# The up scheme on twelve gate tiles instead of eight, one VectorE add for two in each output pair, and half of the last rotation moved back

## The chip, the cores and the metric

The kernel runs on one core of one Trainium2 chip. The metric is device microseconds (us) of one execution. A profiled execution gives a trace, and its *span* is some 1.8 us shorter than the time. TensorE is the matmul engine (PE in the views, PEld its weight loads), VectorE is DVE, ScalarE is ACT, GpSimd is POOL.

## The reference, cut to what matters

The output is `x + A(xn) + B(xn)` with `xn = layernorm(x)`, for 2048 tokens of 512 values:

```python
# A: a diagonal complex state-space layer, B: a gated MLP
for t in range(L):
    h = Lam_bar[None, :] * h + Bu[:, t, :]          # Bu = xn times B_bar
y = 2.0 * einsum("blp,dp->bld", hseq, Cmat).real + x * Dskip
gate, up = xn @ w1, xn @ w3                         # 512 -> 1792 each
out = (silu(gate) * up) @ w2                        # 1792 -> 512
```

Of the kernel before, what the change touches and what calls it, by code (L numbers as in the profile page):

```python
# [11 lines left out]
ALU = mybir.AluOpType  # L12
ACT = mybir.ActivationFunctionType

FP32 = DT.float32
BF16 = DT.bfloat16
FP16 = DT.float16
P = 128
# [4 lines left out]
class Filler:  # L23
# [8 lines left out]
    def add(self, cost, fn, key=None):  # L32
        self.tasks.append((cost, fn, key))
# [30 lines left out]
def kernel(  # L64
# [17 lines left out]
    nc = tc.nc  # L82
    _, S, D = A_x.shape
    F = B_w1.shape[1]
    PS = A_Lambda_re.shape[0]
    CPB = 4
    TBLK = CPB * P
    NCH = S // P
    NBLK = NCH // CPB
# [3 lines left out]
    LN_EPS = 1e-5  # L93
    FIRST = 3
    MID = 8
    NG = 2
    TH = TBLK // 2
    LEAD = 2.0
    LATER = (4, 5)
# [2 lines left out]
    DH = D // 2  # L102
    NFH, NPH = NFT // 2, NPT // 2
    NK = NFH + 2 * NPH
    D1, D2 = slice(0, DH), slice(DH, D)
# [5 lines left out]

    ctx.enter_context(tc.manual_schedule())
    const = ctx.enter_context(tc.tile_pool(name="const", bufs=1))
    xpool = ctx.enter_context(tc.tile_pool(name="xpool", bufs=NBLK))
    lnp = ctx.enter_context(tc.tile_pool(name="lnp", bufs=2))
    xtp = ctx.enter_context(tc.tile_pool(name="xtp", bufs=2))
    glup = ctx.enter_context(tc.tile_pool(name="glup", bufs=3))
# [2 lines left out]
    ssmw = ctx.enter_context(tc.tile_pool(name="ssmw", bufs=2))  # L120
# [26 lines left out]
    tabe = const.tile([P, NPT, 3, TBLK], BF16, name="tabe")  # L147


    x_blk = [xpool.tile([P, CPB, D], BF16, name="x_blk") for _ in range(NBLK)]  # L150
    w1v = B_w1.rearrange("(t p) f -> p t f", p=P)
    w3v = B_w3.rearrange("(t p) f -> p t f", p=P)

# [56 lines left out]
    bg = Filler(LEAD)  # L210
# [99 lines left out]
    gp = nc.gpsimd  # L310
# [112 lines left out]
    def act_state(b, hf):  # L423
        k = k_state(2 * hf)
        return act(b)[:, k:k + 4, :].rearrange("p (j r) t -> p j r t", r=2)
# [21 lines left out]
    def ssm_tasks(b, posts_last=False, between=(), middle=(), late=()):  # L447
        FULL = [P, 2, 2, TBLK]

        def half(hf):  # L450
            psl = slice(2 * hf, 2 * hf + 2)
            st = {}

            def pre_a():
                if b == 0:
                    sin_step((2 * hf + 1, 1))
                    nc.vector.tensor_scalar(out=tabe[:, psl, 2, :], in0=tabe[:, psl, 1, :], scalar1=-1.0,
                                            scalar2=None, op0=ALU.mult)
                st["g"] = u_blk[b, hf]
                if (b, hf) in ((2, 1), (3, 0)):  # L460
                    st["p"] = x_blk[b].rearrange("p (j r) t -> p j r t", r=2)
                elif b == NBLK - 1:
                    st["p"] = xtp.tile([P, NDT, TBLK], BF16, name="xnT").rearrange("p (j r) t -> p j r t", r=2)
                else:
                    st["p"] = ssmw.tile(FULL, BF16, name="p")
                nc.vector.tensor_tensor(out=st["p"][:, :, ::-1, :], in0=st["g"], in1=tabe[:, psl, 2:0:-1, :],
                                        op=ALU.mult)

            def pre_b():
                nc.vector.tensor_tensor(out=st["g"], in0=st["g"], in1=tabe[:, psl, 0:1, :].to_broadcast(FULL),  # L470
                                        op=ALU.mult)

            def pre_c():
                if b == 0 or (b, hf) == (2, 0):
                    nc.vector.tensor_tensor(out=st["g"], in0=st["g"], in1=st["p"], op=ALU.add)
                else:
                    gp.dma_start(out=st["g"], in_=st["p"], accum_op=ALU.add)

            def scan(j, ri):
                pt = 2 * hf + j  # L480
                init = 0.0
                if b in (1, 2):
                    init = ends[:, hf, 2 * j + ri:2 * j + ri + 1]
                elif b > 2:
                    init = act_blk[b - 1][:, k_state(pt, ri), TBLK - 1:TBLK]
                v = st["g"][:, j, ri, :]
                nc.vector.tensor_tensor_scan(out=v, data0=rho[:, pt:pt + 1].to_broadcast([P, TBLK]), data1=v,  # L487
                                             initial=init, op0=ALU.mult, op1=ALU.add)

            def post_a():  # L490
                st["p"] = ssmw.tile(FULL, BF16, name="p")
                st["p16"] = st["p"].bitcast(FP16)
                nc.vector.tensor_tensor(out=st["p16"][:, :, ::-1, :], in0=st["g"], in1=tabe[:, psl, 1:3, :],  # L493
                                        op=ALU.mult)

            def post_b():
                nc.vector.tensor_tensor(out=act_state(b, hf), in0=st["g"],  # L497
                                        in1=tabe[:, psl, 0:1, :].to_broadcast(FULL), op=ALU.mult)

            def post_c():  # L500
                if (b, hf) == (NBLK - 1, 1):
                    nc.vector.tensor_tensor(out=act_state(b, hf), in0=act_state(b, hf), in1=st["p16"], op=ALU.add)
                else:
                    gp.dma_start(out=act_state(b, hf), in_=st["p16"], accum_op=ALU.add)  # L504

            if (b, hf) == (1, 1):
                pre_c.ready = lambda: ("squares", 2, CPB - 1) in sins_done
            pre_a.ready = lambda: (b, hf) in u_blk
            scans = [lambda j=j, ri=ri: scan(j, ri) for j in range(2) for ri in range(2)]
            return (pre_a, pre_b, pre_c), scans, (post_a, post_b, post_c)  # L510

        (pre0, scans0, post0), (pre1, scans1, post1) = (half(hf) for hf in range(NPT // 2))

        transfers = (post0[2],) + (() if b == NBLK - 1 else (post1[2],)) + ((pre1[2],) if b > 0 else ()) + ((pre0[2],) if b in (1, 3) else ())

        def add(*fns):
            for fn in fns:
                bg.add(0.0 if fn in transfers else 1.2, fn, ("scan", b) if fn in scans0 else ("ssm", b))

        if b == 0:  # L520
            add(*pre0, *scans0, *post0, *pre1, *scans1, *post1)
            return
        add(*pre0)
        for t in middle:
            bg.add(*t)
        add(*pre1)
        for t in between:
            bg.add(*t)
        add(*scans0)
        for t in late:  # L530
            bg.add(*t)
        if posts_last:
            add(*scans1)
            return lambda: add(*post0, *post1)
        add(*post0, *scans1, *post1)


    def glu(b):
# [320 lines left out]
        for t in res_list(b):  # L859
            bg.add(*t)  # L860

    def res_difference(b):
        def difference():
            o = xn_blk[b]
            nc.vector.tensor_tensor(out=o[:, 0::2, D2].bitcast(FP16), in0=o[:, 0::2, D2], in1=o[:, 1::2, D2],
                                    op=ALU.subtract)

        bg.add(0.4, difference, ("res", b))

    def weight_state(kh, dsl):  # L870
        return ct[:, kh * NPH:(kh + 1) * NPH, :, dsl].rearrange("p a r d -> p (a r) d")
# [27 lines left out]
    def sum_homes():  # L899
        n = NK * P  # L900
        spare = tw[:, 3, :, :].rearrange("p k d -> p (k d)")
        xs = [x_blk[i].rearrange("p c d -> p (c d)") for i in range(2)]
        q = [v[:, n:n + 2 * DH].bitcast(FP32) for v in xs]
        q.append(const.tile([P, DH], FP32, name="q2"))
        return [[v[:, 0:n] for v in xs], [spare[:, 0:n], spare[:, n:2 * n]]], q

    sums = {}
# [45 lines left out]
    def y_fast(n, then=(), between=()):  # L953
        b, p = pairs[n]
        last = n == len(pairs) - 1
        bg.flush(("sums", n))
        bg.flush("tw")
        if p == 0 and b > 1:
            bg.flush(("scan", b + 1))
        c1 = 2 * p  # L960
        v = sums[n]
        res = xn_blk[b]
        g, halves, f, z = seeded[n]
        q0 = x_blk[2].rearrange("p c d -> p (c d)")[:, 0:2 * DH].bitcast(FP32) if n == 5 else q[0]
        tsum = [weight(0, D2, True)] + [[tw[:, i, k, :] for k in range(NK)] for i in range(3)]
        o1, o2 = res[:, c1, :], res[:, c1 + 1, :]
# [12 lines left out]
        def add(out, x, w):  # L979
            bg.own(0.35)  # L980
            nc.vector.tensor_tensor(out=out, in0=x, in1=w, op=ALU.add)
# [69 lines left out]

        def product7():
            mms(g, v["s3"], tsum[2], False)
            add(o2[:, D1], g, q[2])
            add(o2[:, D2], g, q[1])
            store(c1 + 1, o2)
            if b == 0:
                steps()
                bg.fill()
# [38 lines left out]
    homes, q = sum_homes()  # L1098
# [5 lines left out]
    ln_alloc(2)  # L1104
    for fn in finish_c[:2]:
        bg.add(0.7, fn, "tw")
    res_difference(0)
    first_sums = row_sums(0, *pairs[0])
    for t in first_sums[:2]:
        bg.add(*t)  # L1110
# [28 lines left out]
    sin_step(("norm", 2, CPB - 1))  # L1139
    for cl, o in held:  # L1140
        nc.sync.dma_start(out=ov[:, cl, :], in_=o)
    res_difference(1)
    ssm_tasks(2, between=[(0.2, lambda: keep_ends(1)), *row_sums(2, *pairs[2])], late=res_list(3) + column_sums(3))
    gate = glu(2)
    gate()
    sin_step(("norm", 3, CPB - 1))
    res_difference(2)
    seeds(2)
    bg.flush("cols")
    ssm_tasks(3, middle=[(0.0, after_y2, None), *row_sums(4, *pairs[4])])  # L1150
    res_difference(3)
    keep_ends(1)
    y_fast(2, row_sums(3, *pairs[3]), bu_fast(3, 0))
    y_done.append(2)
# [3 lines left out]
    gate()  # L1158
    for n in range(4, len(pairs)):
        ahead = row_sums(n + 1, *pairs[n + 1]) if n + 1 < len(pairs) else ()  # L1160
        if n == 5:
            for t in ahead:
                bg.add(*t)
        y_fast(n, ahead if n != 5 else ())


# [28 lines left out]
```

## The kernel before: what the change and the argument touch

The kernel works in four blocks of 512 tokens. A block's gates (14 *gate tiles* of 128 features, `silu(gate)*up`) and its rotated states lie in one array `act`. Two *pairs* of 128-token chunks per block, pairs 0 to 7, then turn `act` into output. Many products use a form with seven half-size products instead of eight, paid for with sums of the operands on VectorE and extra moves out of PSUM.

**The up scheme**, in the last block only, does the up side of four gate tiles at a time. `NG` is the number of such groups. Before, `NG = 2`, so eight tiles; the other six take the ordinary route. Calls of the planner (described below) are left out of the listing.

```python
for f in range(4 * NG, NFT):               # ordinary tiles: gate side, up side,
    gate_side(f, tiles[0])                 # 4 matmuls of 512 columns each
    copy(tiles[1][:, f % 2, :], side(w3_sb, f))          # ScalarE empties PSUM
    # ... cut
for n in range(NG):                        # one group: 7 products of 4 x 256 columns
    g, e = (ps_y.tile(...) for _ in range(2))            # the y_ps banks
    f, z = (ps_bu.tile(...) for _ in range(2))
    product(g, a11, b11, True);   copy(f, g)
    product(e, s1n, t1, True);    copy(s5, e)
    gate_side(f0, upper[0])
    product(f, a12, b21, False)
    product(g, s2n, t2, False);   copy(e, g)
    s4n = a12 - s2n                        # VectorE, in place
    copy(upper..., f)
    gate_side(f0 + 1, upper[0])
    product(g, s3n, t3, False);   copy(z, g)
    add(lower..., g)                       # VectorE: PSUM + s5
    product(e, s4n, b22, False)
    add(upper..., e)                       # VectorE: PSUM + s5
    gate_side(f0 + 2, lower[0]); product(z, a22, t4, False); gate_side(f0 + 3, lower[0])
    # ... cut: copies, gates
```

**A pair**, in the order that later blocks use (products 1, 4, 2, 6, 5, 7, 3; for pairs 4 and 5 product 3 runs inside the next pair, after its product 5). The listing goes by number and leaves out products 1 and 2, which need no sum:

```python
sums of act rows, ahead:  s3 = a11 - a21;  s2 = s3 - a22;  s1 = a21 + a22   # VectorE
product4: mms(z, a22, ...); copy(q2, z)       # a22 ends with the block's states
product5: mms(e, s1, ...);  copy(q1, e)
product6: mms(g, s2, ...);  q0 = g + o1[D2]
product7: mms(g, s3, ...);  o2[D1] = g + q2;  o2[D2] = g + q1;  store o2
product3: mms(e, s4, ...);  o1[D2] = e + q0;  store o1
```

**The rotation back** of the states after the scan is three VectorE operations of 2048 elements per half block (`post_a`: p, `post_b`: act, `post_c`: act += p; mostly the last is a transfer, but for the very last half it is a VectorE add). It must be done before the pairs of that block, 6 and 7.

VectorE's background work is put into its queue by a planner in the kernel, `bg`, which keeps an estimate of both engines' time. The order is fixed when the kernel is built, and in the traces VectorE works down that queue: an add at its head waited 0.92 us with ready work behind it (shown below).

## Time and profile before

| | before |
|---|---|
| time, median of 4 runs | 202.25 us (202.14 to 202.29) |
| span of the profiled run | 200.4 us |
| TensorE busy | 195.2 us, 97% |
| VectorE busy | 179.9 us, 90% |
| up scheme, one group (four tiles) | 6.54 us |

A group's time is read from the chain that ended last, listed in order of time (columns: start, length, engine, tile and line, number of matmuls):

```profile
150.91 0.87 PE y_ps L786 x8
...
154.38 0.90 PE y_ps L786 x8
...
160.92 0.90 PE y_ps L786 x8
...
163.98 2.08 PE gu_ps L970 x19
```

Eight matmuls of 256 columns at full pace take 0.87 us. Where the list says 0.90, TensorE lost 0.03 us inside: that is the fourth and fifth product on `g` and `e` of each group. The last line is the first product of pair 4, where the scheme ends.

### The profile page before, as it was taken

Reading aid. Unit: us, or ns where it says so; the run is one execution under the profiler, and the core shown is the slowest. Engines: PE = TensorE matmul, PEld = TensorE weight load, DVE = VectorE, ACT = ScalarE, POOL = GpSimd, SP = SyncE. Lnnn points to the kernel's source line nnn. Section 1 sums busy time; section 2 is a strip of 40 time slices with the busy share of each in tenths; the row PEclk is TensorE's granted clock in tenths of the full one; section 3 lists DMA queues with packets and bytes.
Section 4 is the critical chain, followed back from the end, with each engine's and each line's share of the span. In section 5 each row is a group of like instructions: output and inputs, shape, how many; then the busy total and the mean of one; then the engine's idle time right before and its main releaser. Section 6 shows DMA issues by size and latency. Waiting matters only on the chain.

```text
span 200.4 us, 3599 instructions
## 1 busy us (share of the span) xinstructions
PE 195.2 (97%) x1353; PEld 127.0 (63%) x1365; DVE 179.9 (90%) x257; ACT 133.4 (67%) x275; POOL 50.1 (25%) x71
## 2 busy tenths in 40 slices
PE   7999999999999999999999999999999999999994
PEld 2874444444444488854444468888446678888893
DVE  3699699999999999989999999899989998999732
ACT  4799797799999987967796684362568783111220
POOL 7170279700310142233015013100134003130000
PEclk9999999999999999999999999999999999999999
DMA  6999984990473033945786955550189603974111
GB/s 163 326 273 231 293 162 107 322 295 12 92 151 74 0 65 76 167 118 103 136 145 124 90 105 45 62 130 0 52 170 107 113 0 28 155 75 77 52 41 39
DMA packets 35649, 23.92 MB, mean 119 GB/s; under 512 B 23216, under 2 KB 33584, under 8 KB 35632
## 3 DMA queue, kind: packets, MB, share of 16 engines
q0 software_dynamic: 9520, 10.20, 34.7%
q1 hardware_dynamic: 25536, 13.21, 25.5%
q10 hardware_dynamic: 576, 0.30, 0.6%
q8 instruction: 10, 0.16, 0.4%
q14 instruction: 7, 0.06, 0.1%
HBM read 7.74 MB, written 2.10 MB: 49 GB/s over the span
## 4 chain that ended last, share of the span: by engine, by line
PE 95%; DMA 2%; SPq 1%; issue 0%; DVE 0%
PE gu_ps L544 33%; PE gu_ps L970 17%; PE y_ps L970 10%; PE gu_ps L764 9%; PE bu_ps L970 7%; PE y_ps L439 5%; PE bu_ps L439 5%; PE y_ps L786 2%; DMA w_sb<-in_B_w_dram 2%; PE gu_ps L576 2%; PE gu_ps L689 2%; PE y_ps L689 1%; PE bu_ps L576 1%; PE bu_ps L786 1%; PE bu_ps L689 0%
## 5 line engine op out<-in xcount | busy, mean ns | idle before, releaser
L544 PE MATMUL gu_ps<-xnT,w_sb 128*128 128x512 bf16 x306 | 67.8, 379 | 0.3
L544 PEld LDWEIGHTS <-w_sb 128*128 128x128 bf16 x312 | 30.4, 98 | 36.4
L970 PEld LDWEIGHTS <-act 128*128 128x128 f16 x462 | 43.5, 98 | 5.4
L554 ACT ACTIVATE u<-gu_ps 128x512 bf16<-128x512 f32 x41 | 24.8, 605 | 5.8 <-PE gu_ps L544 5.4
L553 ACT ACTIVATE g<-gu_ps 128x512 bf16<-128x512 f32 x41 | 24.7, 603 | 4.9 <-PE gu_ps L544 4.8
L487 DVE TENSOR_TENSOR_SCAN u<-rho,ends,u 128x512 bf16<-128x512 f32 x16 | 19.9, 1272 | 0.0
L764 PE MATMUL gu_ps<-xnT,w_sb 128*128 128x512 bf16 x77 | 18.4, 379 | 0.2
L504 POOL DMA_DIRECT2D act<-p x7 | 6.4, 909 | 44.2 <-DVE act L497 38.6
L439 PEld LDWEIGHTS <-bt 128*128 128x128 bf16 x96 | 9.4, 98 | 11.3
L970 PE MATMUL gu_ps<-w_sb,act 128*128 128x256 bf16 (+3 forms) x126 | 15.9, 267 | 0.0
L562 DVE TENSOR_TENSOR act<-g,u 128x1024 f16<-128x1024 bf16 x21 | 14.2, 679 | 0.0
L764 PEld LDWEIGHTS <-w_sb 128*128 128x128 bf16 x80 | 7.8, 98 | 7.5
L776 ACT ACTIVATE g<-gu_ps 128x512 bf16<-128x512 f32 x14 | 8.4, 598 | 5.6 <-PE gu_ps L764 5.4
L925 POOL DMA_DIRECT2D act<-act x4 | 7.7, 1929 | 17.5 <-DVE tw L918 15.8
L439 PE MATMUL y_ps<-xnT,bt 128*128 128x512 bf16 x47 | 11.3, 379 | 0.1
L439 PE MATMUL bu_ps<-xnT,bt 128*128 128x512 bf16 x46 | 11.2, 379 | 0.1
L970 PE MATMUL bu_ps<-w_sb,act 128*128 128x256 bf16 (+3 forms) x84 | 10.4, 264 | 0.0
L970 PE MATMUL gu_ps<-ct,act 128*128 128x256 f16 (+1 forms) x72 | 10.4, 267 | 0.0
L470 DVE TENSOR_TENSOR u<-u,tabe 128x2048 bf16<-128x2048 bf16 x8 | 9.8, 1223 | 0.2
L487 DVE TENSOR_TENSOR_SCAN u<-rho,act,u 128x512 bf16<-128x512 f32 x8 | 9.9, 1270 | 0.0
L493 DVE TENSOR_TENSOR p<-u,tabe 128x2048 f16<-128x2048 bf16 x8 | 9.8, 1220 | 0.1
L497 DVE TENSOR_TENSOR act<-u,tabe 128x2048 f16<-128x2048 bf16 x8 | 9.7, 1218 | 0.0
(189 smaller groups left out, 359.0 us busy)
## 6 DMA issues: line engine op xcount, KB each, us to landing
act<-p POOLq DMA_DIRECT2D x7, 512.0 KB, 5.0
xn<-x_blk POOLq DMA_DIRECT2D x4, 512.0 KB, 5.5
out_dram<-xn SPq DMA_DIRECT2D x15, 128.0 KB, 1.7
w_sb<-in_B_w_dram SPq DMA_DIRECT2D x1, 1792.0 KB, 7.9
w_sb<-in_B_w_dram SPq DMA_DIRECT2D x2, 768.0 KB, 6.0
act<-act POOLq DMA_DIRECT2D x4, 352.0 KB, 6.6
w_sb<-in_B_w_dram SPq DMA_DIRECT2D x4, 256.0 KB, 4.5
w_sb<-in_B_w_dram SPq DMA_DIRECT2D x2, 512.0 KB, 5.8
```

Source lines behind the costliest of these rows:

```text
L439: nc.tensor.matmul(out=ps, lhsT=bt[:, ri, dt, pt * P:(pt + 1) * P], rhs=xnT_blk[b][:, dt, :], start=(dt == 0), stop=(dt == NDT - 1))
L470: nc.vector.tensor_tensor(out=st["g"], in0=st["g"], in1=tabe[:, psl, 0:1, :].to_broadcast(FULL), op=ALU.mult)
L487: nc.vector.tensor_tensor_scan(out=v, data0=rho[:, pt:pt + 1].to_broadcast([P, TBLK]), data1=v, initial=init, op0=ALU.mult, op1=ALU.add)
L493: nc.vector.tensor_tensor(out=st["p16"][:, :, ::-1, :], in0=st["g"], in1=tabe[:, psl, 1:3, :], op=ALU.mult)
L497: nc.vector.tensor_tensor(out=act_state(b, hf), in0=st["g"], in1=tabe[:, psl, 0:1, :].to_broadcast(FULL), op=ALU.mult)
L544: nc.tensor.matmul(out=ps[:, tsl], lhsT=w[:, dt, f * P:(f + 1) * P], rhs=xnT[:, dt, tsl], start=(dt == 0), stop=(dt == NDT - 1))
L553: nc.scalar.activation(out=g16[:, f % 2, :], in_=g_ps, func=ACT.Silu)
L554: nc.scalar.activation(out=u16[:, f % 2, :], in_=u_ps, func=ACT.Copy)
L562: nc.vector.tensor_tensor(out=act(b)[:, k0:k1 + 1:k1 - k0, :], in0=g16, in1=u16, op=ALU.mult)
L764: nc.tensor.matmul(out=ps, lhsT=w[:, dt, f * P:(f + 1) * P], rhs=xnT[:, dt, :], start=(dt == 0), stop=(dt == NDT - 1))
L776: nc.scalar.activation(out=g16[:, f % 2, :], in_=side(w1_sb, f), func=ACT.Silu)
L970: nc.tensor.matmul(out=out, lhsT=left[:, k, :], rhs=right[k][:, cols], start=(start and k == 0), stop=(k == NK - 1), skip_group_check=True)
```

## The change

Its intent: fewer TensorE columns (one more group in the up scheme), with VectorE's room made by one add where there were two, and by moving half of the last rotation behind the sums of pair 6. The tiles of x become one tile, so that the two operands of the fused add lie in one access. The core of the diff follows; cuts are marked by "...".

```diff
-    NG = 2
+    NG = 3
...
-    x_blk = [xpool.tile([P, CPB, D], BF16, name="x_blk") for _ in range(NBLK)]
+    x_all = xpool.tile([P, NBLK, CPB, D], BF16, name="x_blk")
+    x_blk = [x_all[:, i] for i in range(NBLK)]
...
-            def post_c():
+            def post_c(tsl=slice(0, TBLK)):          # post_a and post_b likewise
+                a, p16 = act_state(b, hf)[:, :, :, tsl], st["p16"][:, :, :, tsl]
                 if (b, hf) == (NBLK - 1, 1):
-                    nc.vector.tensor_tensor(out=act_state(b, hf), in0=act_state(b, hf), in1=st["p16"], op=ALU.add)
+                    nc.vector.tensor_tensor(out=a, in0=a, in1=p16, op=ALU.add)
...
-        add(*post0, *scans1, *post1)
+        if b < NBLK - 1:
+            add(*post0, *scans1, *post1)
+            return
+        add(*post0, *scans1)
+        early, late = ([(0.6, lambda fn=fn, h=h: fn(slice(h * TH, (h + 1) * TH)), ("ssm", b)) for fn in post1]
+                       for h in range(2))
+        for t in early:
+            bg.add(*t)
+        return late
...
-        q = [v[:, n:n + 2 * DH].bitcast(FP32) for v in xs]
-        q.append(const.tile([P, DH], FP32, name="q2"))
+        both = x_all[:, 0:2].rearrange("p b c d -> p b (c d)")[:, :, n:n + 2 * DH].bitcast(FP32)
+        q = [const.tile([P, DH], FP32, name="q0"), both[:, 1, :], both[:, 0, :], both]
...
             mms(g, v["s3"], tsum[2], False)
-            add(o2[:, D1], g, q[2])
-            add(o2[:, D2], g, q[1])
+            bg.own(0.65)
+            nc.vector.tensor_tensor(out=o2.rearrange("p (h d) -> p h d", h=2),
+                                    in0=g[:, None, :].to_broadcast([P, 2, DH]), in1=q[3], op=ALU.add)
...
-    res_difference(3)                                 # ahead of pair 4
...
-        if n == 5:
+        if n > 4:
             for t in ahead:                           # ahead = sums of pair n + 1
                 bg.add(*t)
-        y_fast(n, ahead if n != 5 else ())
+        if n == 5:
+            for t in (difference(3), *last_posts):    # behind pair 6's sums
+                bg.add(*t)
+        y_fast(n, ahead if n == 4 else ())
```

More of the change, by code (lines that the diff above doesn't have):

```diff
@@ L113 @@
     const = ctx.enter_context(tc.tile_pool(name="const", bufs=1))
-    xpool = ctx.enter_context(tc.tile_pool(name="xpool", bufs=NBLK))
+    xpool = ctx.enter_context(tc.tile_pool(name="xpool", bufs=1))
     lnp = ctx.enter_context(tc.tile_pool(name="lnp", bufs=2))
@@ L488, in scan, with post_a, post_b @@
                                              initial=init, op0=ALU.mult, op1=ALU.add)
-            def post_a():
-                st["p"] = ssmw.tile(FULL, BF16, name="p")
-                st["p16"] = st["p"].bitcast(FP16)
-                nc.vector.tensor_tensor(out=st["p16"][:, :, ::-1, :], in0=st["g"], in1=tabe[:, psl, 1:3, :],
+            def post_a(tsl=slice(0, TBLK)):
+                if "p16" not in st:
+                    st["p16"] = ssmw.tile(FULL, BF16, name="p").bitcast(FP16)
+                nc.vector.tensor_tensor(out=st["p16"][:, :, ::-1, tsl], in0=st["g"][:, :, :, tsl],
+                                        in1=tabe[:, psl, 1:3, tsl], op=ALU.mult)
+            def post_b(tsl=slice(0, TBLK)):
+                nc.vector.tensor_tensor(out=act_state(b, hf)[:, :, :, tsl], in0=st["g"][:, :, :, tsl],
+                                        in1=tabe[:, psl, 0:1, tsl].to_broadcast([P, 2, 2, tsl.stop - tsl.start]),
                                         op=ALU.mult)
-            def post_b():
-                nc.vector.tensor_tensor(out=act_state(b, hf), in0=st["g"],
-                                        in1=tabe[:, psl, 0:1, :].to_broadcast(FULL), op=ALU.mult)
-            def post_c():
+            def post_c(tsl=slice(0, TBLK)):
+                a, p16 = act_state(b, hf)[:, :, :, tsl], st["p16"][:, :, :, tsl]
                 if (b, hf) == (NBLK - 1, 1):
-                    nc.vector.tensor_tensor(out=act_state(b, hf), in0=act_state(b, hf), in1=st["p16"], op=ALU.add)
+                    nc.vector.tensor_tensor(out=a, in0=a, in1=p16, op=ALU.add)
                 else:
-                    gp.dma_start(out=act_state(b, hf), in_=st["p16"], accum_op=ALU.add)
+                    gp.dma_start(out=a, in_=p16, accum_op=ALU.add)
             if (b, hf) == (1, 1):
@@ L860, in res_tasks, with difference, run @@
             bg.add(*t)
-    def res_difference(b):
-        def difference():
+    def difference(b):
+        def run():
             o = xn_blk[b]
@@ L866, in difference @@
                                     op=ALU.subtract)
-        bg.add(0.4, difference, ("res", b))
+        return 0.4, run, ("difference", b)
     def weight_state(kh, dsl):
@@ L957, in y_fast @@
         bg.flush("tw")
+        bg.flush(("difference", b))
         if p == 0 and b > 1:
@@ L1106 @@
         bg.add(0.7, fn, "tw")
-    res_difference(0)
+    bg.add(*difference(0))
     first_sums = row_sums(0, *pairs[0])
@@ L1141 @@
         nc.sync.dma_start(out=ov[:, cl, :], in_=o)
-    res_difference(1)
+    bg.add(*difference(1))
     ssm_tasks(2, between=[(0.2, lambda: keep_ends(1)), *row_sums(2, *pairs[2])], late=res_list(3) + column_sums(3))
@@ L1146 @@
     sin_step(("norm", 3, CPB - 1))
-    res_difference(2)
+    bg.add(*difference(2))
     seeds(2)
     bg.flush("cols")
-    ssm_tasks(3, middle=[(0.0, after_y2, None), *row_sums(4, *pairs[4])])
-    res_difference(3)
+    last_posts = ssm_tasks(3, middle=[(0.0, after_y2, None), *row_sums(4, *pairs[4])])
     keep_ends(1)
```

## The prediction

> **What bounds the kernel now.** I read the busy times first, then the chain that ended last, then a table of busy time by stage, then the order in time of TensorE and VectorE near the end. The page's first and fourth parts:
>
> ```profile
> PE 195.2 (97%) x1353; PEld 127.0 (63%) x1365; DVE 179.9 (90%) x257; ACT 133.4 (67%) x275; POOL 50.1 (25%) x71
> ...
> PE 95%; DMA 2%; SPq 1%; issue 0%; DVE 0%
> ```
>
> The chain is TensorE for 95% of the span, and VectorE has no share in it, although it is 90% busy. A busy TensorE need not be at its peak, so I looked at the pace: in the chain of waits, in order of time, eleven matmuls of 256 columns advance it by 1.20 us (109 ns each), and four of 512 columns by 0.86 us (216 ns each). From 13 us to the last product I find no step off that pace but one of 0.03 us in each of the two groups of the up scheme. So the time is a sum of matmul columns: what TensorE doesn't do is gained, what makes it wait is lost. The last block's gate and up stage and the pairs after it, in a table of stretches (columns: stretch, length, busy us with counts of PE, PEld, DVE, ACT, POOL, then granted clock, DMA share, GB/s):
>
> ```profile
> 140.40:150.70 10.30, 10.25 (x49) 4.69 (x48) 9.22 (x12) 6.57 (x11) 2.90 (x3) 1.00 0.54 115
> 150.70:157.30 6.60, 6.55 (x45) 4.32 (x45) 6.59 (x9) 5.36 (x10) 1.66 (x2) 1.00 1.15 131
> 157.30:163.80 6.50, 6.45 (x44) 4.29 (x44) 6.42 (x8) 5.34 (x10) 0.00 (x0) 1.00 0.14 26
> 163.80:171.00 7.20, 7.20 (x67) 6.44 (x66) 6.46 (x9) 2.91 (x9) 2.01 (x2) 1.00 0.39 30
> 171.00:179.40 8.40, 8.40 (x79) 7.54 (x78) 8.40 (x12) 1.72 (x5) 2.77 (x2) 1.00 0.88 117
> 179.40:189.00 9.60, 9.60 (x90) 8.57 (x89) 9.34 (x16) 1.81 (x6) 0.00 (x0) 1.00 0.42 65
> 189.00:198.00 9.00, 8.66 (x101) 7.85 (x99) 3.29 (x8) 1.31 (x4) 0.00 (x0) 1.00 0.11 37
> ```
>
> The reader is to see three things: the clock is full everywhere; VectorE is full in the up scheme (150.7 to 163.8) and in pairs 5 and 6 (171 to 189); and it has 5.7 us to spare after 189. The first row is six ordinary gate tiles, rows two and three are one group of four tiles each in the seven-product up scheme.
>
> **What the Trainium skill says.** "TensorE: Matmul & The Clock Gate", section "Wait — 56ns, not 53.3ns?": warm matmuls start N / 2.4 GHz plus about 2.5 ns apart, 215.7 ns at 512 columns. The trace agrees at both sizes (216 and 109 ns; the formula gives 109.2 at 256). The same page, "Back-to-back issue gap", says that in a real stream 512 columns take about 131 ns; this trace does not agree. "VectorE: DVE Perf Modes", "The perf-mode tier table": a two-tensor operation on 16-bit SBUF data runs at twice the rate, with any PSUM operand at the single rate. The rows agree: 1024 16-bit elements take 685 ns, 512 from PSUM 677 ns. "Perfetto Trace Analysis", "Matmuls": groups should rotate through PSUM banks so that emptying one overlaps the next. That is what can break here: the scheme has two banks (y_ps) that VectorE must empty before the next group writes them.
>
> **The change part by part.** The costs of the operations that it multiplies:
>
> ```profile
> L796 DVE TENSOR_TENSOR u<-y_ps,bt 128x512 bf16<-128x512 f32 x4 | 2.5, 677 | 0.0
> L827 DVE TENSOR_TENSOR w_sb<-w_sb,bt 128x512 f16<-128x512 bf16 x2 | 0.8, 416 | 0.0
> L750 DVE TENSOR_TENSOR bt<-w_sb 128x1024 f16<-128x1024 bf16 x1 | 0.7, 682 | 0.0
> L981 DVE TENSOR_TENSOR xn<-gu_ps,q 128x256 bf16<-128x256 f32 x4 | 1.7, 418 | 1.0 <-PE gu_ps L970 1.0
> L502 DVE TENSOR_TENSOR act<-act,p 128x2048 f16<-128x2048 f16 x1 | 1.2, 1217 | 0.0
> ```
>
> 1. Twelve gate tiles in the up scheme, not eight. Four ordinary tiles' up sides, 16 matmuls of 512 columns, become 28 of 256. TensorE: 16 x 0.2157 = 3.45 us out, 28 x 0.1092 = 3.06 us in, plus the 0.03 us step that each group shows (a product that waits for a ScalarE copy). Check from the time order: the groups begin at 150.74 and 157.28, so one takes 6.54 us; four ordinary tiles take 8 x 0.863 = 6.90. Gain: **0.36 us**, all on the path.
> VectorE gets more: three sums of 1536 elements instead of 1024 (from 685 ns at 1024 and 885 at 1408, some 0.95 us each: +0.27 x 3 = 0.8), one more in-place difference and two more PSUM adds. VectorE starts the next operation about 0.08 us before the listed end of the last, so these take 0.33 + 2 x 0.60 = 1.5. Together +2.3 us, in a stage that is full. ScalarE gets six copies for four, +1.2 us; it is at 5.3 of 6.5 in a group already, so it holds.
> 2. The quarters q1 and q2 side by side: two adds of 256 become one of 512, with the PSUM operand read twice. 2 x 418 ns become about 677 (the form of the L796 row): 0.16 us of VectorE for each of 8 pairs (0.08 by start-to-start), nothing for TensorE. It is not at the end: in the last pair product 7 comes before product 3, and the last add is of 128 columns, released by TensorE; its 0.29 us and the store after it stay.
> 3. The last block's second half of the rotation back (p, act and their sum, three of 1.22 us) in two time halves; the later one goes behind pair 6's sums, with the difference of block 3 (0.42 us). Each of six halves costs about 0.68 us by the 1024 row, so 6 x 0.6 for 3 x 1.14 by start-to-start: +0.2 us in all, but 1.8 us leave the full stretch before pair 6 for the stretch where VectorE has room. Before, the sum of this half ended at 180.19 and pair 6 needs it at 180.63:
>
> ```profile
> 178.97 1.22 DVE L502 TENSOR_TENSOR act<-act,p 128x2048 f16<-128x2048 f16 x1
> ...
> 182.02 0.89 DVE L918 TENSOR_TENSOR x_blk<-x_blk,act 128x1408 f16<-128x1408 f16 x1
> ```
>
> and the second sum of pair 6 ended at 182.91, just ahead of the product that reads it at 183.03. So before has only 0.1 us to spare there; this part makes the room that part 1's extra VectorE work takes.
>
> Sum on the path: -0.36, 0 and 0. That is 202.28 - 0.36 = 201.92 if nothing waits.
>
> **Does TensorE wait?** In the changed instruction order the first rotation (p) of the last block moves from the scheme into pair 4 (1.15 us out of the stage), and only two ordinary tiles stand before the scheme. I laid the listed order on the durations above; it is an estimate by hand:
> - First group, from about 143.83. The sums s1, s3, s2 run 140.9 to 143.7; the first of them is needed at 144.3, the last at 146.0. Good. The difference s4 ends at about 147.3 and is needed at 147.8.
> - Second group, from 150.37. The first y_ps bank is free by 149.9; the second by 150.4, needed at 150.8. Its s4 stands behind two adds, a gate, a pair sum, a rotation and a gate; it ends at about 154.0, and its weight load is due at 154.2. Here there is no more than **0.1 to 0.2 us** to spare.
> - Third group, from 156.9: s4 ends at 160.4, needed at 160.8.
> - Pair 4's s4 sum can start at about 167.0 (before: at 167.62, after waiting 0.56 us for TensorE), pair 6's sums end at 181.3 instead of 182.9, pair 7's at 191, needed at 191.9.
>
> I add 0.03 us for such waits as an expectation: **201.95 us**.
>
> **The rivals.** (a) VectorE becomes the bound in the up scheme: s4 or a y_ps bank comes late in one group and TensorE stops for 0.1 to 0.5 us. For it: busy 6.59 of 6.60 us in the second row, and +2.3 us more. Against: the moved rotation and the fused adds. The time would be 202.0 to 202.4, the gain gone. (b) TensorE never waits and the fused adds shorten the end as well: 201.8. Against: in the order of time the last adds wait for TensorE, not for VectorE. (c) A rotation half too late for pair 7: its a22 is needed at about 190.0. By my layout the late half's sum ends at 187.5, so 2 us to spare; it would cost up to 1 us if the order in pair 6 were wrong. (d) The one tile for all of x brings waits that were not there. In the listed waits I see none new that matters; unlikely.
>
> **Range and chances.** The gain is 0.36 us, under 0.2% of the time, and the runs of before lie within 0.06 us. Below, 201.75 would need a gain that I don't see; above, 202.3 is a stop of some 0.4 us in the scheme. 201.75 to 202.3 should hold it 8 times in 10. Two per cent is 4 us: nothing in either direction is of that size, so within 2% has 0.98, faster and slower 0.01 each.
>
> **What would show it right or wrong.** Right: TensorE's busy time falls by some 0.4 us of span; matmuls of the gate stage fall by 16 and the scheme's rise by 28; the three groups take 6.54 us each; VectorE's chain share stays 0%; the fused add is about 0.68 us. Wrong: a TensorE idle ahead of the scheme's weight loads released by VectorE; a group longer than 6.6 us; the chain with VectorE in it around 147 to 161 us or at pair 7; or a fused add at well over 0.7 us, which would put VectorE's room in doubt.

## The result, and the profile after

| | before | changed |
|---|---|---|
| median of 4 runs | 202.25 us (202.14 to 202.29) | 201.94 us (201.55 to 202.03) |
| the same again, other runs | 202.30 us (9 runs, 202.00 to 202.89) | 201.92 us (5 runs, 201.73 to 202.40) |
| span of the profiled run | 200.4 us | 200.1 us |

What I expected of the second set of runs of the changed kernel:

> The changed kernel once more, with five rounds, to pin the gain: 0.36 us of TensorE columns say 0.3 to 0.4 us below before, ratio 0.9982; its groups of the scheme take 6.51 to 6.54 us with no stop but the 0.03 us steps. If the start of the kernel varies between runs, single times scatter by more than the gain and the stretch from the scheme on is what repeats.

The ratio is 0.9982 (95% interval 0.9965 to 0.9999), and 0.9984 (0.9970 to 0.9997) the second time. It is some 0.3 us faster.

The page of the changed kernel, busy times and shares of the chain:

```profile
PE 196.5 (98%) x1377; PEld 128.6 (64%) x1377; DVE 181.9 (91%) x255; ACT 133.9 (67%) x277; POOL 49.8 (25%) x71
...
PE 96%; DMA 1%; DVE 1%; SPq 0%; issue 0%; DVEq 0%
```

TensorE's busy time is *higher* than before although it has fewer columns to work: before has 1353 matmul records, 12 fewer than it issued. Busy sums with records missing can't show a gain of 0.4 us. VectorE's 1% of the chain looks like a new wait, but in the order of time it all lies in the first 6 us and the last 0.3 us: this run's chain starts at the load of x and its statistics, the run of before at a weight load. From 6.7 us to the last add the chain is TensorE alone, and in the second trace of the changed kernel the page gives VectorE 0%.

The gate and up stage and pair 6, from the table of stretches (columns as in the prediction):

```profile
143.80:150.30 6.50, 6.50 (x46) 4.27 (x45) 6.50 (x10) 5.27 (x11) 1.71 (x2) 1.00 0.43 81
150.30:156.90 6.60, 6.60 (x46) 4.33 (x45) 6.35 (x10) 5.42 (x11) 2.85 (x2) 1.00 1.17 136
156.90:163.40 6.50, 6.50 (x46) 4.27 (x44) 6.42 (x9) 5.32 (x11) 0.00 (x0) 1.00 0.43 81
...
188.60:197.70 9.10, 8.79 (x103) 7.98 (x100) 5.70 (x10) 1.30 (x4) 0.00 (x0) 1.00 0.12 39
```

Three groups stand where there were two, VectorE is full in each, and TensorE is too. In the last stretch VectorE went from 3.29 busy us to 5.70. That is not the moved half rotation itself, which ran from 185.22 to 187.59 us, but pair 7's three sums, which it pushed back: they started at 189.31 where before they started at 185.10. The chain in order of time:

```profile
140.65 3.45 PE gu_ps L775 x16
144.10 0.87 PE y_ps L797 x8
...
160.64 0.90 PE y_ps L797 x8
...
163.70 2.40 PE gu_ps L982 x22
```

Two ordinary tiles (16 matmuls) and then three groups. The scheme ended at 163.98 before and at 163.70 now.

**What repeats and what doesn't.** The gain is smaller than the scatter of single runs (0.15 to 1.25 us within one set; one single run of the kernel before, taken beside the last experiment, gave 202.92). The traces say where the scatter is: the last product of pair 3, up to which TensorE does the same work in all the kernels below, starts anywhere from 139.05 to 139.61 us. What comes after it repeats to 0.02 us. So I read each trace in two stretches, from the start records of TensorE and VectorE (a record of a first matmul starts some 0.17 us before its piece in the chain):

- S1, from that start to the first matmul of pair 4 (the stage with the up scheme);
- S2, from there to the start of the last add on VectorE (pairs 4 to 7).

The three records of each, first of the kernel before, then of the changed one:

```profile
139.18 0.93 PE L970 MATMUL bu_ps<-w_sb,act 128*128 128x256 bf16 x7
163.82 0.93 PE L970 MATMUL gu_ps<-w_sb,act 128*128 128x256 bf16 x7
197.70 0.29 DVE L981 TENSOR_TENSOR xn<-gu_ps,x_blk 128x128 bf16<-128x128 f32 x1 [0.20 <-PE gu_ps L970]
...
139.28 0.93 PE L982 MATMUL bu_ps<-w_sb,act 128*128 128x256 bf16 x7
163.54 0.93 PE L982 MATMUL gu_ps<-w_sb,act 128*128 128x256 bf16 x7
197.43 0.29 DVE L993 TENSOR_TENSOR xn<-gu_ps,q 128x128 bf16<-128x128 f32 x1 [0.27 <-PE gu_ps L982]
```

| kernel | S1 | S2 | sum | against before |
|---|---|---|---|---|
| before | 24.64 | 33.88 | 58.52 | |
| changed | 24.26 | 33.89 | 58.15 | -0.37 |
| changed, again | 24.25 | 33.91 | 58.16 | -0.36 |

The whole gain is in S1, 0.38 us, and it is repeated to 0.01.

### The profile page after: what moved, and what is told of

Same layout as the page of the kernel before. It is cut to its first block, busy times and chain, and to the rows that moved or that the text cites. A ratio compares the mean times of both kernels' runs of the same rounds, so it can differ in the third digit from the quotient of the medians.

```text
span 200.1 us, 3642 instructions
## 1 busy us (share of the span) xinstructions
PE 196.5 (98%) x1377; PEld 128.6 (64%) x1377; DVE 181.9 (91%) x255; ACT 133.9 (67%) x277; POOL 49.8 (25%) x71
## 4 chain that ended last, share of the span: by engine, by line
PE 96%; DMA 1%; DVE 1%; SPq 0%; issue 0%; DVEq 0%
PE gu_ps L555 34%; PE gu_ps L982 17%; PE y_ps L982 10%; PE gu_ps L775 7%; PE bu_ps L982 7%; PE y_ps L440 5%; PE bu_ps L440 5%; PE y_ps L797 3%; PE gu_ps L587 2%; PE gu_ps L700 2%; DMA x_blk<-in_A_x_dram 1%; PE bu_ps L797 1%; PE y_ps L700 1%; PE bu_ps L587 1%; PE y_ps L243 1%; PE bu_ps L700 0%
## 5 line engine op out<-in xcount | busy, mean ns | idle before, releaser
L555 PE MATMUL gu_ps<-xnT,w_sb 128*128 128x512 bf16 x312 | 68.2, 379 | 0.0
L555 PEld LDWEIGHTS <-w_sb 128*128 128x128 bf16 x312 | 30.4, 98 | 36.5
L775 PE MATMUL gu_ps<-xnT,w_sb 128*128 128x512 bf16 x64 | 15.9, 379 | 0.0
L1005 ACT ACTIVATE x_blk<-gu_ps 128x256 f32<-128x256 f32 (+1 forms) x9 | 3.3, 367 | 10.6 <-PE gu_ps L982 10.6
L494 DVE TENSOR_TENSOR p<-u,tabe 128x2048 f16<-128x2048 bf16 (+1 forms) x9 | 9.9, 1099 | 0.1
L498 DVE TENSOR_TENSOR act<-u,tabe 128x2048 f16<-128x2048 bf16 (+1 forms) x9 | 9.9, 1097 | 0.0
```

The lines of the kernel that those rows point to most:

```text
L494: nc.vector.tensor_tensor(out=st["p16"][:, :, ::-1, tsl], in0=st["g"][:, :, :, tsl], in1=tabe[:, psl, 1:3, tsl], op=ALU.mult)
L498: nc.vector.tensor_tensor(out=act_state(b, hf)[:, :, :, tsl], in0=st["g"][:, :, :, tsl], in1=tabe[:, psl, 0:1, tsl].to_broadcast([P, 2, 2, ...
L555: nc.tensor.matmul(out=ps[:, tsl], lhsT=w[:, dt, f * P:(f + 1) * P], rhs=xnT[:, dt, tsl], start=(dt == 0), stop=(dt == NDT - 1))
L775: nc.tensor.matmul(out=ps, lhsT=w[:, dt, f * P:(f + 1) * P], rhs=xnT[:, dt, :], start=(dt == 0), stop=(dt == NDT - 1))
```

## The experiments

The theory (A) was: TensorE sets the time by its columns, so the third group gives 0.38 us; but only because the other two parts keep VectorE in time. The rivals: (B) the columns alone decide and the other parts do nothing; (C) the other parts are worth something of their own. All kernels gave a correct result. Their S1 and S2 stand in one table at the end of this section.

### The third group alone

```diff
 # the kernel before
-    NG = 2
+    NG = 3
```

> The kernel before with twelve tiles in the up scheme and nothing else. Theory A (TensorE is the sum of its columns only as long as VectorE keeps up; the moved rotation and the fused adds pay for the scheme's VectorE work): VectorE comes to pair 6 about 1.9 us late (three halves of 0.54 us and the difference of 0.34 us stand before its sums again, where the changed kernel had no time left), TensorE stops there in products 4 and 6 for 1.5 to 2.0 us together, and the time is 203.4 to 204.0. Theory B (the columns alone decide, the other parts do nothing): 201.9, no stop of TensorE, like the changed kernel.

Measured: 204.72 us, median of 4 (204.41 to 205.05), ratio 1.0121 (1.0100 to 1.0142): slower than before. S1 is 24.25, all of the gain, and S2 is 36.29, a loss of 2.41 us. TensorE in order of time shows where (in brackets: idle before it, and what released it):

```profile
180.13 0.93 PE L970 MATMUL gu_ps<-tw,act 128*128 128x256 f16 x7
182.22 0.61 PE L970 MATMUL gu_ps<-tw,act 128*128 128x256 f16 x4 [1.16 <-DVE act L502]
...
184.94 1.37 PE L970 MATMUL gu_ps<-tw,x_blk 128*128 128x256 f16 x11 [0.91 <-DVE x_blk L918]
```

Product 4 of pair 6 runs its first seven matmuls, whose weights are gates, then stops for the four whose weights are the states that the rotation makes; product 6 then stops for the second sum. The idle time in brackets starts at the modelled end of a matmul; from start to start the two stops are 1.33 and 1.07 us, together the 2.40. The reader sees two things. VectorE's extra work in the scheme (2.3 us by the prediction's estimate) didn't hurt in the scheme, but 17 us later: the first rotation (L493), which before ran inside the scheme at 161.35, now ran at 168.66, and against the start of pair 4 the second sum of pair 6 ended 2.47 us later. And the time limit of the rotation is at the eighth matmul of product 4, not at its first. B falls. The stop was longer than I expected (1.5 to 2.0), and the time above my range.

### The other two parts alone

```diff
 # the changed kernel
-    NG = 3
+    NG = 2
```

> The changed kernel with eight tiles in the scheme as before: only the fused add and the split rotation are left. Theory A: no column of TensorE is saved, so the time is that of before, 202.2 to 202.3, with VectorE's sums for pair 6 done over 1 us ahead of need. Theory C (the fused adds or the split are worth something by themselves, at the end of the kernel or at pair 6): 201.9 to 202.1.

Measured: 202.18 us, median of 4 (202.11 to 202.50), ratio 0.9998 (0.9980 to 1.0016); S1 24.63, S2 33.88, as before. Pair 6's second sum ended at 180.27, over two us earlier than in the kernel before (182.91), and TensorE gained nothing from it:

```profile
179.39 0.88 DVE L929 TENSOR_TENSOR x_blk<-x_blk,act 128x1408 f16<-128x1408 f16 x1
```

C falls. The parts are worth nothing apart; together with the third group they are worth 2.4 us.

### The rotation whole again

```diff
 # the changed kernel
-        if b < NBLK - 1:
+        if True:                      # all posts in place, none late
             add(*post0, *scans1, *post1)
             return
...
+    bg.add(*difference(3))            # ahead of pair 4, as before
...
-            for t in (difference(3), *last_posts):
-                bg.add(*t)            # and the sums of pair 7 not queued ahead
```

> The changed kernel with the last rotation whole again, and the difference of block 3 where it was, both ahead of pair 6's sums; scheme on twelve tiles and fused adds stay. Theory A: as in the scheme alone, a stop of 1.4 to 1.9 us at pair 6, time 203.3 to 203.8. Theory B: 201.9.

Measured: 204.19 us, median of 4 (203.88 to 204.58), ratio 1.0095 (1.0074 to 1.0116); S2 35.95. The stop is 35.95 - 33.89 = 2.06 us, a little over what was expected (the time too), at the same two places in pair 6:

```profile
183.07 0.61 PE L982 MATMUL gu_ps<-tw,act 128*128 128x256 f16 x4 [1.48 <-DVE act L505]
...
185.14 1.38 PE L982 MATMUL gu_ps<-tw,x_blk 128*128 128x256 f16 x11 [0.25 <-DVE x_blk L929]
```

This run also puts the difference of block 3 back ahead of the sums. That alone costs 0.35 us (below), so some 1.7 us of the 2.06 are the rotation's, if the two simply add.

### Two adds again

```diff
 # the changed kernel, product 7
-            bg.own(0.65)
-            nc.vector.tensor_tensor(out=o2..., in0=g[:, None, :].to_broadcast([P, 2, DH]), in1=q[3], op=ALU.add)
+            add(o2[:, D1], g, q[2])
+            add(o2[:, D2], g, q[1])
```

> The changed kernel with the last quarters in two VectorE operations again. Theory A: VectorE reaches pair 6's sums 0.1 to 0.3 us later, and as they ended just when TensorE needed them, TensorE stops for about that long: 202.0 to 202.2. Rival (the fused add matters not at all): 201.9, no stop at pair 6 beyond the 0.02 us that the changed kernel shows.

Measured: 202.15 us, median of 4 (202.03 to 202.89), ratio 1.0002 (0.9974 to 1.0031), which settles nothing. The trace does: S1 24.25, S2 34.24, a stop of 0.35 us at pair 6, almost the whole gain and a little over the 0.1 to 0.3 expected. It is also twice the 0.16 us that the adds of pairs 4 and 5 save by start-to-start. The planner also put the third scan behind an add that waits 0.16 us for TensorE; in the changed kernel the scan fills that wait. So part of the 0.35 is probably the order that came with the edit, not the add itself; no run separates the two.

### The room in the scheme

```diff
 # the changed kernel, ahead of s4 in each group
+            if n == 1:      # the result is not used; the target is a finished weight tile
+                nc.vector.tensor_tensor(out=w1_sb[:, 0:2, 12 * P:14 * P].bitcast(FP16), in0=a12, in1=s2n, op=ALU.subtract)
             nc.vector.tensor_tensor(out=s4n, in0=a12, in1=s2n, op=ALU.subtract)
```

> The changed kernel with one more VectorE operation of 0.42 us (0.34 by start-to-start) just ahead of s4 in the second group; its result is not used, the output stays right. If the room there is 0.1 to 0.2 us as predicted, TensorE stops for 0.15 to 0.25 us before the product that reads s4, and the group takes 6.7 to 6.8 us instead of 6.54. If VectorE has much more room there, no stop.

Measured in one look: 202.55 us, S1 24.56, S2 33.90. S1 grew by 0.31 us, more than expected, because the probe cost VectorE more than I had reckoned: s4 began 0.51 us later (14.93 against 14.42 us after the last product of pair 3). It is written in place over what the probe reads, and it started 0.52 us after the probe (154.01), not 0.34. 0.51 - 0.31 leaves 0.20 us of room, the upper edge of what the prediction said. Once more the chain names it:

```profile
154.53 0.44 DVE w_sb L840
...
155.02 0.61 PE y_ps L797 x4
```

### The difference ahead again, and where VectorE's room goes

First the difference of block 3 alone goes back ahead of pair 6's sums:

```diff
 # the changed kernel
+    bg.add(*difference(3))                            # ahead of pair 4
...
-            for t in (difference(3), *last_posts):
+            for t in last_posts:
```

> The changed kernel with the difference of block 3 (0.34 us of VectorE) back ahead of pair 6's sums; the rotation stays split. In the changed kernel the second sum ended just as TensorE needed it (a step of 0.02 us), so all of the 0.34 us should show as a stop before product 6 of pair 6: 0.3 to 0.35 us, time about 202.3. If there was hidden room, less.

Measured: 202.02 us, under the 202.3 expected, with the earliest start of pair 3's last product (139.05); S2 34.24, a stop of 0.35 us where 0.30 to 0.35 was expected. The changed kernel has no room there at all. I had laid out 1.4 us (sums done at 181.3, product 6 due at about 182.7), so I looked for what I had missed. VectorE in order of time in the changed kernel:

```profile
168.88 1.22 DVE L494 TENSOR_TENSOR p<-u,tabe 128x2048 f16<-128x2048 bf16 x1
171.01 0.69 DVE L1067 TENSOR_TENSOR xn<-gu_ps,x_blk 128x512 bf16<-128x512 f32 x1 [0.92 <-PE gu_ps L982]
171.62 1.22 DVE L498 TENSOR_TENSOR act<-u,tabe 128x2048 f16<-128x2048 bf16 x1
...
178.15 0.42 DVE L993 TENSOR_TENSOR xn<-gu_ps,q 128x256 bf16<-128x256 f32 x1
...
180.29 0.68 DVE L505 TENSOR_TENSOR act<-act,p 128x1024 f16<-128x1024 f16 x1
180.89 0.88 DVE L929 TENSOR_TENSOR x_blk<-act 128x1408 f16<-128x1408 f16 x1
181.81 0.89 DVE L929 TENSOR_TENSOR x_blk<-x_blk,act 128x1408 f16<-128x1408 f16 x1
```

At 171.01 the fused add of pair 4 sat at the head of VectorE's queue for 0.92 us, waiting for product 7, with ready work behind it. The obvious repair is to put the ready operation (L498) ahead of it, with the difference still ahead of pair 6:

```diff
             if n in LATER:
-                bg.fill()
+                bg.fill(3.2 if (n, i) == (4, 5) else None)
```

> The changed kernel with the difference of block 3 ahead of pair 6's sums, which made TensorE stop for 0.35 us, and with the 1.22 us operation ahead of the fused add of pair 4. If the lost room came from that wait, the 0.9 us that it frees cover the 0.34 us of the difference, and the stop is gone; if VectorE merely waits later instead, the stop stays at 0.35 us.

Measured: 202.10 us; S2 34.23, the stop is still 0.34 us. The wait of 0.92 us was gone, but two others took its place, the second being

```profile
177.99 0.42 DVE L993 TENSOR_TENSOR xn<-gu_ps,q 128x256 bf16<-128x256 f32 x1 [0.48 <-PE gu_ps L982]
```

(0.34 us more at 174.38). My first explanation fell. The add at 177.99 waits for product 3 of pair 4. It can't start before TensorE gets there, and only what stands behind it in the queue (two rotations, the fused add of pair 5, the rotation's sum, the difference, two sums) decides when pair 6 is served. Room that VectorE gains ahead of that add is lost at it. So, as the next step, the first half rotation (L494) goes ahead of that add:

```diff
+                if n == 5:
+                    bg.fill(2.6)
                 later.pop(n - 1)()        # product 3 of pair 4 and its add
```

> As the run before (the difference ahead of pair 6's sums, the 1.22 us operation ahead of pair 4's fused add), and one more move: the first half rotation (0.68 us) ahead of the add after product 3 of pair 4, which waited 0.48 us for TensorE with the half rotation behind it in the queue. The run before showed that room freed ahead of that add is lost at it. If that add is what starts the last stretch of VectorE to pair 6, moving work ahead of it frees about 0.45 us, more than the 0.35 us that TensorE stopped: no stop at pair 6. If the stretch starts later than that add, the stop stays at 0.35 us.

Measured: 201.96 us; S2 33.96. Of the stop of 0.34 us, 0.07 are left, so nearly all of it is gone:

```profile
177.68 0.69 DVE L494 TENSOR_TENSOR p<-u,tabe 128x1024 f16<-128x1024 bf16 x1
178.28 0.42 DVE L993 TENSOR_TENSOR xn<-gu_ps,q 128x256 bf16<-128x256 f32 x1
```

The add no longer waits. The sums' end moved by 0.27 us rather than by the 0.45 expected, because the next add in the queue waits in its turn: the fused add of pair 5 started at 179.39, 0.11 us after product 7 of pair 5 ended in the chain (179.28). The fused add of pair 4 follows its product by the same 0.1 us in the changed kernel (171.01 after 170.91).

### The step of 0.03 us in each group

```diff
 # the changed kernel, in each group
-            product(f, a12, b21, False)
             product(g, s2n, t2, False)
             copy(e, g)
+            product(f, a12, b21, False)
```

> The changed kernel with the order of two products in each group of the scheme turned round, so that the ScalarE copy that product 7 waits for gets 0.44 us more. My reading of the 0.03 us step in each group (the product waits for that copy) says that the steps go, 0.02 + 0.03 + 0.03 = 0.07 us: 201.87 where the changed kernel has 201.94, seen in the trace rather than in the times. If the step is something else (a bank, the weight load), it stays.

Measured: 201.77 us, median of 5 (201.62 to 202.22), ratio to before 0.9978 (0.9964 to 0.9992); S1 24.19, S2 33.90. The chain has no 0.90 left in the scheme; all groups take 6.51 us:

```profile
144.05 0.87 PE y_ps L797 x8
...
160.54 0.87 PE y_ps L797 x8
...
163.58 2.51 PE gu_ps L982 x23
```

So the step was the wait for the ScalarE copy: in the changed kernel the second group's copy ended at 153.91 and the product that needs it started at 153.97. This version beats before by its own interval, and the changed kernel by 0.06 us in the traces; by the times alone those two can't be told apart. Adding to it the first repair above (L498 earlier), which leaves the difference behind pair 6's sums:

> The turned product order of the run before, and in pair 4 the 1.22 us operation that stood in VectorE's queue behind the fused add (which waited 0.92 us for TensorE) moved ahead of that add. If that wait is where VectorE lost its room, pair 6's second sum ends 0.6 to 0.9 us earlier, the last step of TensorE (0.02 us at pair 6) goes too, and the time is 201.8, 0.1 below the changed kernel and 0.45 below before. No more than that: no column is saved.

Measured: 202.01 us, median of 6 (201.35 to 202.60), ratio 0.9990 (0.9971 to 1.0010): unclear by time. In the trace S1 is 24.18 and S2 33.90, the same as without the repair, and pair 6's second sum ended no earlier against the start of pair 4 (182.58 - 163.42 = 19.16 us, and 182.70 - 163.54 = 19.16 in the changed kernel). The expectation of 0.6 to 0.9 us was wrong, for the reason just given.

| kernel | S1 | S2 | lost to a stop, against changed |
|---|---|---|---|
| third group alone | 24.25 | 36.29 | 2.40 at pair 6 |
| no third group | 24.63 | 33.88 | none; 0.37 of columns |
| rotation whole | 24.25 | 35.95 | 2.06 at pair 6 |
| two adds | 24.25 | 34.24 | 0.35 at pair 6 |
| probe in the scheme | 24.56 | 33.90 | 0.31 in the second group |
| difference ahead | 24.25 | 34.24 | 0.35 at pair 6 |
| difference ahead, L498 earlier | 24.26 | 34.23 | 0.34 at pair 6 |
| the same, L494 earlier too | 24.26 | 33.96 | 0.07 |
| product order | 24.19 | 33.90 | gains 0.07 in S1 |
| product order, L498 earlier | 24.18 | 33.90 | gains 0.08 in S1 |

## Why the prediction was right, point by point

- **What bounds it: right.** TensorE's columns set the time before and after; S1 fell by 0.38 us and S2 stayed. The agreement of 201.94 with the 201.95 predicted is closer than the scatter of the start allows anyone to claim; the 0.38 of the trace is the better proof.
- **The gain of the third group, 0.36: right, slightly under-sized.** It was 0.38 us. 16 x 0.2157 - 28 x 0.1092 is 0.39; I took 0.03 off for the added group's step, and the changed kernel's first group (0.89 us for eight matmuls) lost only 0.02. The rest is within the 0.02 to which the stretches repeat.
- **VectorE's cost in the scheme: right.** The sums of 1536 elements took 0.948 to 0.958 us (0.95 foreseen), the adds 0.68. My order by hand was within 0.35 us of the trace through the three groups: s4 of the second group ended at 154.12 (about 154.0 foreseen), and 0.20 us of room was left (0.1 to 0.2 foreseen).
- **The fused add: right in its cost, wrong in "nothing for TensorE".** It took 0.683 to 0.692 us (0.677 foreseen). Without it TensorE stops for 0.35 us at pair 6. "Sum on the path: -0.36, 0 and 0" holds for the three parts together but not one by one: parts 2 and 3 are worth nothing without the third group and carry it when it is there. For part 3 the prediction said so ("this part makes the room"); for part 2 it named relief in the scheme only (rival (a)), not at pair 6.
- **Pair 6: wrong in two steps.** "Before, the sum of this half ended at 180.19 and pair 6 needs it at 180.63" put the need at the first matmul of product 4; it is at the eighth, 0.76 us later (seven matmuls at 0.109), as the run with the third group alone shows. And "pair 6's sums end at 181.3 instead of 182.9" came out as 182.70: the layout has no wait of VectorE for TensorE in pair 4, where the trace has 0.92 us of it at the fused add. The other 0.5 us of the miss is not accounted for. The room there was not 1.4 us but none; TensorE lost 0.02 us at it:

```profile
182.75 1.38 PE L982 MATMUL gu_ps<-tw,x_blk 128*128 128x256 f16 x11
```

  The product before it in the same bank took 1.36. That the total held in spite of this is luck of 0.3 us: with the difference left ahead it would have been a stop.
- **Rival (a)**, a late s4 or bank in the scheme, didn't happen; the probe shows that it was 0.20 us away. **(b)**, a shorter end, didn't: S2 is unchanged. **(c)**, pair 7 too late, didn't: no stop of TensorE at pair 7 in any trace. **(d)**, new waits from the single tile for x: none seen; S2 of the kernel without the third group, which has that tile, is that of before.
- **The signs named:** VectorE's share of the chain went to 1%, which I had called a sign of a stop; here it was the start of the run. TensorE's busy time didn't fall, because records were missing before. Both were poor signs for a gain this small. The 0.06 us within which the runs of before were said to lie was three runs; all those named here spread from 201.88 to 202.92.

## What to carry to other kernels

When one engine runs without a gap, a gain in its work is worth what it says only if every other engine still delivers in time, and the bill can come due far from the stage where the work was added: here some 2.3 us (an estimate) of VectorE in one stage became 2.4 us of TensorE stop 17 us later. To find the room, follow the queue back from the delivery to the last operation that had to wait for the bound engine: only work behind that operation counts, and room gained ahead of it is lost at it. For a gain below the scatter of whole runs, compare stretches of the traces between two instructions that both kernels have.

## What the Trainium skill lacked or had wrong

- "TensorE: Matmul & The Clock Gate", "Back-to-back issue gap", gives some 131 ns for 512 columns and 81 ns for 128 in a real stream of weight loads and matmuls. Here such a stream ran at 216 ns for 512 columns (3.45 us for 16), 109 for 256 and 55 for 128 (0.61 us for 11): the page's formula for a single gap holds, its figures for a stream don't.
- No page has the consequence of VectorE's fixed order that decided here: where an operation at the head of its queue waits for TensorE with ready work behind it (0.92 us at pair 4), moving that work ahead gains nothing if a later operation in the queue waits again (0.34 and 0.48 us; the stop stayed at 0.34).
